# Five row chunks of 512, 512, 384, 384, 384 instead of four of 512 and one of 128, with operands moved to one offset modulo 64 bytes

## The chip, the core and the metric

The kernel runs on one core of a Trainium2 chip. The time is the device time of one execution in microseconds (us); the kernel before takes 840.11 us, the median of three runs (839.91 to 841.11). TensorE (PE) multiplies, VectorE (DVE), ScalarE (ACT) and GpSimd (POOL) work elementwise, and all DMAs are issued from SyncE (SP). A matmul on PE is a pair: a weight load (LDWEIGHTS, shown as engine PEld) of a stationary 128x128 block, and the MATMUL itself, which streams the columns of the moving operand through it.

## The reference

Four batches of 544 tokens (32 global, 512 local), eight heads of 64. Attention, then two feed-forward blocks over all 2176 tokens:

```
x  = attention(...)                      # local: window of 32 and the 32 globals; global: all keys
h  = x @ w_in                            # 512 -> 2048     "first"
g  = h * clip(h + 3, 0, 6) / 6
y  = g @ w_out                           # 2048 -> 512     "second"
h2 = max(y @ w1, y @ w2, y @ w3)         # 512 -> 768, x3  "third"
out = h2 @ w_out                         # 768 -> 512      "fourth"
```

The arithmetic is float32 where attention works on it; the four products split each operand into two fp32r parts (hi and lo) and add three products, hi·hi, hi·lo and lo·hi. The weights arrive as 64-bit floats and are decoded on the chip.

## The kernel before

Tokens are worked in chunks of rows (`CHUNKS`): four of 512, which are the local tokens of one batch each, and one of 128, the global tokens of all four batches. A product works with tokens as columns of its moving operand, so the chunk's length is the column count n of every MATMUL of the first three products: `first` and `second` issue 12 of them for each of 16 blocks f, `third` 12 for each of 18 blocks, in each chunk. That is 192, 192 and 216 pairs of load and matmul a chunk, whatever n is. `fourth` takes 18 MATMULs of 512 columns for every 128 tokens, 306 in all.

Work is recorded as operations with an engine, an assumed length, a due time and the buffers that they touch, and `Plan.order` deals them out to the engines; what it fixes is the order on each engine, no time. Attention goes by pairs of heads (`pair`) and for the global tokens by two pairs (`globals_`). Attention's results are split into the parts of x by x_hi on ACT (L337) and x_lo on DVE (L339), into tiles xt (two buffers, one batch each), and by g_hi and g_lo (L400, L402) into xg. `first` (L450) leaves each block in DRAM (gs); `second` (L538) loads it again (gr), splits it (g2: L529, L531) and sums over f in four banks; its results are the tiles y. `third` is L590, `fourth` L614, the stores L625 and L628.

`decode` loads a weight block into raw, works it on ACT (L427), DVE (L418, L420, L423) and ACT (L431), and POOL writes the low part (L432). Its results lie in two rings, w with 16 places and wx with 8: w_in's sixteen blocks take w, w_out's first eight take wx, its last eight the places of w that `first` has left. Of the last two products' 24 blocks the first eight go to w, the next eight to wx, the last eight to w.

In the program as built, the tiles w, wx, g2 and hs (the split result of `third`) begin at a multiple of 64 bytes in each partition, the tiles xt, xg and y at 32 bytes past one. All blocks inside a tile lie whole multiples of 64 bytes further on. So in `first` and `third` the moving operand (xt, xg, y) and the weights stand 32 bytes apart modulo 64; in `second` (moving g2, weights w or wx) and `fourth` (moving w, weights hs) they stand at the same offset, 0.

Of the kernel before, what the change touches and what calls it, by code (L numbers as in the profile page):

```python
# [28 lines left out]
CHUNKS = [(0, 512), (512, 512), (1024, 512), (1536, 512), (2048, 128)]  # L29
# [134 lines left out]
def body(ctx, tc, q_n, k_n, v_r, msk, msk_g, w_in, w_out, w123, w_out2, out):  # L164
# [10 lines left out]
    pools["wx"] = ctx.enter_context(P("wx", 8))  # L175
# [7 lines left out]
    tiny = const.tile([128, 1], F32, name="tiny")  # L183
    nc.vector.memset(tiny, 1.0e-9)
# [48 lines left out]
    T["wx"] = tag("wx", 8, [128, 2, 512], F32R, "wx")  # L233
# [7 lines left out]
    xT = {b: Buf(T["xt"]) for b in range(B)}  # L241
# [6 lines left out]
    def pair(b, pr, s0):  # L248
# [3 lines left out]
        xt = xT[b]  # L252
# [8 lines left out]
        for u in range(2):  # L261
# [12 lines left out]
            op("PE", 0.70, scores, s0 + 2 * u, r=[Q, K], w=sb + [(t, "held") for t in tb], what="scores")  # L274
# [28 lines left out]
            for hh in range(2):  # L303
                fb, pt = Buf(T["f"]), Buf(T["pt"])
                pts.append(pt)
                def norm(hh=hh, tb=tb, nm=nm):
                    t = tb[hh]()[:, :, 0:WIN]
                    r = nm()[:, 2, hh].rearrange("p (v o) -> p v o", o=1).to_broadcast([128, 2, WIN])
                    nc.gpsimd.tensor_tensor(out=t, in0=t, in1=r, op=ALU.mult)  # L309

                op("POOL", 1.25, norm, s0 + 2 * u + 4, r=[(nm, 2)], w=[(tb[hh], 0), (tb[hh], 1)], what="norm")
# [23 lines left out]
            op("PE", 0.9, pv, s0 + 2 * u + 7, r=pts + [V], w=[(ob, u)], what="pv")  # L335
# [3 lines left out]
        op("DVE", 0.7, lambda: nc.vector.tensor_tensor(out=xt()[:, 1, pr], in0=ob(), in1=xt()[:, 0, pr].bitcast(F32),  # L339
                                                       op=ALU.subtract), s0 + 11, r=[ob, (xt, (0, pr))],  # L340
           w=[(xt, (1, pr))], what="x_lo")

    def globals_(b, pr, g0):
# [46 lines left out]
        def g_pv():  # L390
# [9 lines left out]
        op("ACT", 0.28, lambda: nc.scalar.copy(out=xG()[:, 0, pr - 1:pr + 1, b], in_=ogv()), g0 + 10, r=[og],  # L400
           w=[(xG, (0, b, pr))], what="g_hi")
        op("DVE", 0.28, lambda: nc.vector.tensor_tensor(  # L402
            out=xG()[:, 1, pr - 1:pr + 1, b], in0=ogv(), in1=xG()[:, 0, pr - 1:pr + 1, b].bitcast(F32),
            op=ALU.subtract), g0 + 11, r=[og, (xG, (0, b, pr))], w=[(xG, (1, b, pr))], what="g_lo")

    def decode(src, into, due, rel=0.0):
# [22 lines left out]
        for i in range(3):  # L429
            op("DVE", (0.6, 0.75, 0.85)[i], lambda i=i: bits(i), due + 3, r=[R], w=[t_], what="wbits")  # L430
# [37 lines left out]
    for b in range(B + 1):  # L468
        if b < B:
            for pr in range(H // 2):  # L470
# [5 lines left out]
                s += 8 if b else 6  # L476
# [21 lines left out]
    plan.event(end_of_attention, ("att", "psS", "psF", "psO"), ("psA", "gp"))  # L498
# [22 lines left out]
    def second(c, f, due):  # L521
# [9 lines left out]
        op("DVE", 0.15 + n * .0012, lambda: nc.vector.tensor_tensor(  # L531
# [29 lines left out]
    for n in range(3 * NH + NH):  # L561
# [5 lines left out]
        W = decode(src, "wx" if 8 <= n < 16 else "w", s2 + 20 + 12 * n if n < 8 else s3 + 2.5 * (n - 8))  # L567
# [39 lines left out]
    def fourth(c, due):  # L607
# [88 lines left out]
```

## Time and profile before

| | |
|---|---|
| median of three runs | 840.11 us |
| the profiled execution: its time / its span | 840.04 / 838.3 us |
| granted TensorE clock, mean | 0.998 |
| attention alone | 0 to 53 us |
| attention and `first` together | 53 to 245 us |
| `first` alone, then with the first blocks of `second` | 245 to 354 us |
| `second` alone | 354 to 519 us |
| `second`'s chunk of 128 and `third` | 519 to 549 us |
| `third` and `fourth` | 549 to 834 us |

The span runs from the first instruction to the last; 1.7 us of the time lie outside it. The boundaries of the stages are where the first and the last MATMUL of a line start. A share of busy time of PE counts overlapping matmuls once and says nothing on how close together they are; for that the start of one group of matmuls is set against the start of the next.

### The profile page before, as it was taken

What the parts mean: (1) busy time and instruction counts of PE and PEld (TensorE: products, weight loads), DVE (VectorE), ACT (ScalarE), POOL (GpSimd) and SP (SyncE); (2) the same over time, 40 slices, a digit from 0 to 9 for tenths busy, and PEclk for the clock granted to TensorE, in tenths of its full rate; (3) what the DMA queues carried; (4) which work ended last, traced back from release to release, by engine and by line L of the source; (5) the groups of instructions that cost most, each with busy time, mean ns of one, the idle gap of its engine ahead of it and who ended that gap; (6) DMA issues with size and microseconds to landing.
All of it is one profiled execution on the core that took longest, in us unless ns stands there. A gap on an engine that the chain in (4) does not pass through costs nothing.

```text
span 838.3 us, 12516 instructions
## 1 busy us (share of the span) xinstructions
PE 822.4 (98%) x4754; PEld 671.1 (80%) x4754; DVE 374.6 (45%) x832; ACT 322.3 (38%) x754; POOL 140.2 (17%) x134
## 2 busy tenths in 40 slices
PE   6989999999999999999999999999999999999997
PEld 4767777777888888888888888988888888888897
DVE  3687878768333465643232322588122122112111
ACT  5987777776333444423232323344111111111101
POOL 2564445435000132300000001233000000000000
PEclk9999999999999999999999999999999999999999
DMA  6255746444433456643333330343100100000010
GB/s 234 69 187 191 240 125 217 160 128 152 151 115 128 134 163 202 187 144 101 94 95 101 96 94 28 99 126 100 51 1 0 38 13 0 26 26 2 13 38 13
DMA packets 53916, 85.61 MB, mean 102 GB/s; under 512 B 4576, under 2 KB 26336, under 8 KB 53856
## 3 DMA queue, kind: packets, MB, share of 16 engines
q1 hardware_dynamic: 53856, 84.81, 31.8%
q8 instruction: 37, 0.61, 0.3%
q14 instruction: 23, 0.19, 0.1%
HBM read 62.51 MB, written 22.28 MB: 101 GB/s over the span
## 4 chain that ended last, share of the span: by engine, by line
PE 96%; ACT 2%; DVE 1%; DMA 0%; POOL 0%; issue 0%; SPq 0%; ACTq 0%
PE l L450 24%; PE a L590 17%; PE a L538 16%; PE l L590 10%; PE l L538 8%; PE a L614 5%; PE f L316 4%; PE o L330 3%; PE s L271 3%; PE l L614 3%; PE s L355 1%; PE o L396 1%; ACT tbuf L284 1%; PE f L381 1%; DMA kr<-in_kn_dram 0%; ACT pt L246 0%
## 5 line engine op out<-in xcount | busy, mean ns | idle before, releaser
L450 PE MATMUL l<-xt,w 128*128 128x512 f32 x768 | 193.3, 401 | 0.0
L450 PEld LDWEIGHTS l<-xt,w 128*128 128x128 f32 x768 | 140.0, 188 | 36.1 <-issue 5.0
L531 DVE TENSOR_TENSOR g<-gr,g 128x512 fp32r<-128x512 f32 (+1 forms) x80 | 49.2, 616 | 126.0 <-ACT g L529 125.9
L529 ACT CAST g<-gr 128x512 fp32r<-128x512 f32 (+1 forms) x80 | 44.5, 558 | 137.3 <-PE a L538 70.9
L432 POOL TENSOR_TENSOR w<-wdec,w 128x512 fp32r<-128x512 f32 x40 | 54.6, 1365 | 175.2 <-ACT w L431 173.8
L456 ACT ACTIVATE ga<-l,three 128x512 f32<-128x512 f32 x80 | 49.7, 622 | 88.6 <-PE l L450 87.8
L590 PE MATMUL a<-y,w 128*128 128x512 f32 (+1 forms) x372 | 80.0, 372 | 0.0
L458 DVE SCALAR_TENSOR_TENSOR ga<-ga,l 128x512 f32<-128x512 f32 x80 | 48.3, 605 | 67.0 <-ACT ga L456 66.8
L590 PEld LDWEIGHTS a<-y,w 128*128 128x128 f32 x372 | 64.4, 188 | 13.6
L309 POOL TENSOR_TENSOR tbuf<-tbuf,nm 128x448 f32<-128x448 f32 x64 | 63.9, 1018 | 59.6 <-DVE nm L297 42.5
L538 PE MATMUL a<-g,wx 128*128 128x512 f32 (+1 forms) x336 | 69.4, 357 | 0.0
L538 PE MATMUL a<-g,w 128*128 128x512 f32 (+1 forms) x336 | 68.4, 356 | 0.0
L601 ACT CAST hs<-hm 128x512 fp32r<-128x512 f32 (+1 forms) x30 | 16.7, 556 | 125.9 <-DVE hm L599 125.9
L590 PE MATMUL a<-y,wx 128*128 128x512 f32 (+1 forms) x300 | 64.0, 371 | 0.0
L538 PEld LDWEIGHTS a<-g,w 128*128 128x128 f32 x336 | 56.2, 189 | 9.5
L538 PEld LDWEIGHTS a<-g,wx 128*128 128x128 f32 x336 | 55.9, 189 | 9.3
L284 ACT ACTIVATE tbuf<-tbuf,nm 128x224 f32<-128x224 f32 x128 | 60.4, 476 | 6.9 <-DVE nm L278 6.9
L590 PEld LDWEIGHTS a<-y,wx 128*128 128x128 f32 x300 | 51.8, 188 | 11.0
L599 DVE TENSOR_TENSOR hm<-hm,a 128x512 f32<-128x512 f32 (+1 forms) x37 | 22.6, 611 | 78.4 <-PE a L590 78.3
L432 POOL TENSOR_TENSOR wx<-wdec,wx 128x512 fp32r<-128x512 f32 x16 | 21.0, 1318 | 213.7 <-ACT wx L431 213.7
L278 DVE CUSTOM_DVE_ANT_0 tbuf<-s,mask 128x224 f32<-128x224 f32 x128 | 43.5, 384 | 22.2 <-PE s L271 20.6
L423 DVE SCALAR_TENSOR_TENSOR wdec<-raw,wdec 128x512 int32<-128x512 int32 x56 | 49.2, 879 | 1.0
(72 smaller groups left out, 1080.0 us busy)
## 6 DMA issues: line engine op xcount, KB each, us to landing
gs<-ga SPq DMA_DIRECT2D x64, 256.0 KB, 2.4
gr<-gs SPq DMA_DIRECT2D x64, 256.0 KB, 2.6
raw<-in_w_out_dram SPq DMA_DIRECT2D x22, 512.0 KB, 3.7
raw<-in_w_dram SPq DMA_DIRECT2D x18, 512.0 KB, 3.7
raw<-in_w_in_dram SPq DMA_DIRECT2D x16, 512.0 KB, 3.9
vr<-in_v_dram SPq DMA_DIRECT2D x16, 320.0 KB, 5.4
kr<-in_kn_dram SPq DMA_DIRECT2D x16, 304.0 KB, 4.8
qr<-in_qn_dram SPq DMA_DIRECT2D x16, 288.0 KB, 3.8
```

What stands on the lines that cost most here:

```text
L284: nc.scalar.activation(out=t, in_=t, func=ACTF.Exp, scale=-1.0, bias=nm()[:, 0, hh, v:v + 1], accum_out=nm()[:, 1, hh, v:v + 1])
L309: nc.gpsimd.tensor_tensor(out=t, in0=t, in1=r, op=ALU.mult)
L423: nc.vector.scalar_tensor_tensor(out=t, in0=half(0), scalar=29, in1=t, op0=ALU.logical_shift_right, op1=ALU.bitwise_or)
L432: op("POOL", 1.36, lambda: nc.gpsimd.tensor_tensor(out=flat(1), in0=t_().bitcast(F32), in1=flat(0).bitcast(F32), op=ALU.subtract), due + 5 ...
L450: nc.tensor.matmul(ps()[:, 0:n], lhsT=w[:, i, k], rhs=v, start=(k == 0 and s == 0), stop=(k == KC - 1 and s == 2))
L456: op("ACT", us, lambda: nc.scalar.activation(out=ga()[:, 0:n], in_=ps()[:, 0:n], func=ACTF.Relu, bias=three), -100, r=[ps], w=[ga], what=" ...
L458: op("DVE", us, lambda: nc.vector.scalar_tensor_tensor(out=ga()[:, 0:n], in0=ga()[:, 0:n], scalar=6.0, in1=ps()[:, 0:n], op0=ALU.min, op1= ...
L529: op("ACT", 0.16 + n * .0009, lambda: nc.scalar.copy(out=g2()[:, 0, 0:n], in_=gr()[:, 0:n]), due - 4, r=[gr], w=[(g2, 0)], what="ghi")
L531: op("DVE", 0.15 + n * .0012, lambda: nc.vector.tensor_tensor(out=g2()[:, 1, 0:n], in0=gr()[:, 0:n], in1=g2()[:, 0, 0:n].bitcast(F32), op= ...
L538: nc.tensor.matmul(A[e]()[:, 0:n], lhsT=wo[f]()[:, i, e * 128:(e + 1) * 128], rhs=g2()[:, j, 0:n], start=(f == 0 and s == 0), stop=(f == N ...
L590: nc.tensor.matmul(U[j]()[:, 0:n], lhsT=w[:, i, k], rhs=y[c]()[:, l, k], start=(s == 0), stop=(s == len(steps) - 1))
L614: nc.tensor.matmul(A[i](), lhsT=h2[c, h]()[:, p, i * 128:(i + 1) * 128], rhs=w4[h]()[:, l], start=(h == 0 and s == 0), stop=(h == NH - 1 a ...
```

## The change

`CHUNKS` becomes 512, 512, 384, 384, 384. Chunk 2 is the first 384 local rows of batch 2, chunk 3 the last 128 of batch 2 and the first 256 of batch 3, chunk 4 the last 256 of batch 3 and the 128 global rows. A head pair's result is therefore split in up to two pieces, each into the x tile of its chunk (L337/L339 become L348/L350, 24 of each in place of 16), and there are three x tiles, not two. The global rows are collected in one float32 tile xg (`g_x`) and split into chunk 4's x once, after the last of them. For room, wx has four places instead of eight, and a ring wy of four is opened where attention's space is given back: w_out's first four blocks take wx, the twelve others w as `first` leaves it; the third product's blocks 0 to 3 take w, 4 to 7 wy, 8 to 11 wx, the rest w.

A tile `pad` of 32 bytes in the constants' pool moves what is allocated on that side by 32 bytes: w, wx, wy, g2 and hs now begin at 32 past a multiple of 64 bytes, as xt and y do. In the program as built all four products have both operands at offset 32.

The planner's due times of the head pairs are set further apart (8 and then 16 where it had 6 and 8), and some of its assumed lengths are changed; these only move the order. All of the first product's chunks 3 and 4 are now due after attention.

```diff
-CHUNKS = [(0, 512), (512, 512), (1024, 512), (1536, 512), (2048, 128)]
+CHUNKS = [(0, 512), (512, 512), (1024, 384), (1408, 384), (1792, 384)]
...
-    pools["wx"] = ctx.enter_context(P("wx", 8))
+    pools["wx"] = ctx.enter_context(P("wx", 4))
...
+    const.tile([128, 8], F32, name="pad")
...
-    T["xt"] = tag("xt", 2, [128, 2, KC, SL], F32R, "lp")
-    T["xg"] = tag("xg", 1, [128, 2, KC, B, SG], F32R, "lp")
+    T["xt"] = tag("xt", 3, [128, 2, KC, 512], F32R, "lp")
+    T["xg"] = tag("xg", 1, [128, KC, B, SG], F32, "lp")
...
-        op("ACT", 0.6, lambda: nc.scalar.copy(out=xt()[:, 0, pr], in_=ob()), s0 + 10, r=[ob], w=[(xt, (0, pr))],
-           what="x_hi")
+        for c, (t0, n) in enumerate(CHUNKS):
+            i0, i1 = max(t0, b * SL) - b * SL, min(t0 + n, b * SL + SL) - b * SL
+            if i0 >= i1:
+                continue
+            at = b * SL + i0 - t0
+            xv = lambda l, c=c, at=at, m=i1 - i0: X[c]()[:, l, pr, at:at + m]
+            src = lambda i0=i0, i1=i1: ob()[:, i0:i1]
...
-                s += 8 if b else 6
+                s += 16 if b else 8
...
-        else:
+        elif b < B:
             for f in range(NF):
                 first(b - 1, f, due1)
                 due1 += 3
-                if b == B:
-                    first(B, f, due1)
-                    due1 += 1
+    c = len(CHUNKS) - 1
+    at = CHUNKS[c][1] - B * SG
+    xg = lambda: xG().rearrange("p k b q -> p k (b q)")
+    op("ACT", 0.6, lambda: nc.scalar.copy(out=X[c]()[:, 0, :, at:at + B * SG], in_=xg()), due1, r=[xG], w=[(X[c], (0, "g"))], what="g_hi")
...
+    for c in range(B - 1, len(CHUNKS)):
+        for f in range(NF):
+            first(c, f, due1)
+            due1 += 3
...
+        pools["wy"] = ctx.enter_context(P("wy", 4))
...
-        wo[f] = decode(src, "wx" if f < 8 else "w", s2 - 50 + 3 * f)
+        wo[f] = decode(src, "wx" if f < 4 else "w", s2 - 50 + 3 * f)
...
-        W = decode(src, "wx" if 8 <= n < 16 else "w", s2 + 20 + 12 * n if n < 8 else s3 + 2.5 * (n - 8))
+        W = decode(src, ("w", "wy", "wx", "w", "w", "w")[n // 4], s2 + 20 + 12 * n if n < 8 else s3 + 2.5 * (n - 8))
```

How the order moves on PE, at three places. Names: s scores, f transposes of the softmax ("flips"), o attention's output, l and a banks of the products. First the start, where attention gives way to the first matmuls of `first`. Before:

```order
L271 MATMUL s<-kr,qr 128x224 x4
L330 MATMUL o<-pt,vr 64x128 x16
L316 MATMUL f<-ident,tbuf_118 128x128 x4
L316 MATMUL f<-ident,tbuf_120 128x128 x4
L271 MATMUL s<-kr,qr 128x224 x4
L316 MATMUL f<-ident,tbuf_122 128x128 x4
L330 MATMUL o<-pt,vr 64x128 x8
L316 MATMUL f<-ident,tbuf_124 128x128 x4
L381 MATMUL f<-ident,tg 128x128 x4
L450 MATMUL l<-xt,w 128x512 x6
```

After, at the same place:

```order
L273 MATMUL s<-kr,qr 128x224 x4
L318 MATMUL f<-ident,tbuf_115 128x128 x4
L318 MATMUL f<-ident,tbuf_117 128x128 x4
L332 MATMUL o<-pt,vr 64x128 x16
L273 MATMUL s<-kr,qr 128x224 x4
L456 MATMUL l<-xt,w 128x512 x24
L273 MATMUL s<-kr,qr 128x224 x4
L456 MATMUL l<-xt,w 128x512 x6
L318 MATMUL f<-ident,tbuf_119 128x128 x4
```

Ahead of the first matmul of `first` stood 20 flips of four and 12 groups of scores; now 16 and 10, which is batch 0 and little more.

The end of `first` and the start of `second`, on PE. Before:

```order
L396 MATMUL o<-pt,vr 64x32 x20
L450 MATMUL l<-xt,w 128x512 x144
L450 MATMUL l<-xg,w 128x128 x12
L450 MATMUL l<-xt,w 128x512 x12
L450 MATMUL l<-xg,w 128x128 x12
```

After:

```order
L392 MATMUL f<-ident,tg 128x128 x5
L456 MATMUL l<-xt,w 128x384 x12
L407 MATMUL o<-pt,vr 64x32 x20
L456 MATMUL l<-xt,w 128x384 x492
L554 MATMUL a<-g_2924,wx 128x512 x12
L554 MATMUL a<-g_2935,wx 128x512 x12
L554 MATMUL a<-g_2949,wx 128x512 x12
```

Chunks of 512 and 128 alternated there, with four blocks of `second` between them further on; now 492 matmuls of 384 columns stand in a row, and `second` begins after the last.

The end of `second` and the start of `third`, on PE. Before:

```order
L538 MATMUL l<-g_4873,w 128x512 x9
L538 MATMUL a<-g_4890,wx 128x128 x12
L538 MATMUL a<-g_4907,wx 128x128 x12
L590 MATMUL a<-y_4073,w 128x512 x12
L538 MATMUL a<-g_4961,wx 128x128 x12
L538 MATMUL a<-g_4963,wx 128x128 x12
L538 MATMUL a<-g_4966,wx 128x128 x12
L538 MATMUL a<-g_5006,wx 128x128 x12
L590 MATMUL l<-y_4073,w 128x512 x12
```

After:

```order
L554 MATMUL a<-g_5185,w 128x384 x12
L554 MATMUL a<-g_5202,w 128x384 x12
L554 MATMUL a<-g_5222,w 128x384 x12
L606 MATMUL a<-y_4053,w 128x512 x12
L606 MATMUL l<-y_4053,w 128x512 x36
L606 MATMUL a<-y_4053,wy 128x512 x48
L606 MATMUL a<-y_4053,wx 128x512 x12
```

Blocks of `third` no longer stand between `second`'s last ones; `third` begins when all of them are done.

## Rows read from the trace of the kernel before

**Rows 1.** The page: granted clock in 40 slices, chain by engine.
```profile
PEclk9999999999999999999999999999999999999999
...
PE 96%; ACT 2%; DVE 1%; DMA 0%; POOL 0%; issue 0%; SPq 0%; ACTq 0%
```

**Rows 2.** What PE waited for: total us, times, longest.
```profile
PE s L271 <- DMA kr<-in_kn_dram: 4.5, 1, 4.5
PE s L271 <- DVE nm L278: 2.5, 2, 1.4
PE o L330 <- DVE xt L339: 1.0, 1, 1.0
PE f L316 <- ACT pt L246: 1.0, 1, 1.0
```

**Rows 3.** Chain of waits in order of time: start, us, engine, out, line, instructions.
```profile
429.85 44.20 PE a L538 x195
...
530.52 6.65 PE a L538 x60
...
635.83 8.40 PE l L590 x36
...
788.95 16.36 PE a L614 x72
...
810.61 6.70 PE a L590 x60
```

**Rows 4.** Timeline of PE where `first` runs alone: start us, us, instructions.
```profile
245.37 33.86 PE L450 MATMUL l<-xt,w 128*128 128x512 f32 x144
279.08 1.45 PE L450 MATMUL l<-xg,w 128*128 128x128 f32 x12
280.37 3.01 PE L450 MATMUL l<-xt,w 128*128 128x512 f32 x12
283.21 1.45 PE L450 MATMUL l<-xg,w 128*128 128x128 f32 x12
```

**Rows 5.** Timeline of PE, two short windows of one group of scores.
```profile
100.30 0.35 PE L271 MATMUL s<-kr,qr 64*128 64x224 f32 x2
...
100.68 0.35 PE L271 MATMUL s<-kr,qr 64*128 64x224 f32 x2
```

**Rows 6.** Timeline of PE and of PEld, from `first` into a flip.
```profile
142.48 0.63 PE L450 MATMUL l<-xt,w 128*128 128x512 f32 x2
142.94 0.49 PE L316 MATMUL f<-ident,tbuf 128*128 128x128 f32 x3
...
142.71 0.59 PEld L316 LDWEIGHTS f<-ident,tbuf 128*128 128x128 f32 x4
```

**Rows 7.** Timeline of PE: `first` between pieces of attention.
```profile
53.23 1.64 PE L450 MATMUL l<-xt,w 128*128 128x512 f32 x6
54.71 0.27 PE L381 MATMUL f<-ident,tg 128*128 128x128 f32 x1
...
56.96 1.66 PE L450 MATMUL l<-xt,w 128*128 128x512 f32 x6
58.55 1.36 PE L396 MATMUL o<-pt,vr 128*64 128x32 f32 x40
```

**Rows 8.** Stretches: busy PE, PEld, DVE, ACT, POOL; clock; DMA share, GB/s.
```profile
40.00:60.00 20.00, 17.40 (x204) 13.52 (x201) 16.39 (x50) 16.90 (x53) 11.22 (x10) 1.00 0.54 177
80.00:100.00 20.00, 20.00 (x163) 15.03 (x161) 18.34 (x37) 14.63 (x37) 10.87 (x10) 1.00 0.69 213
```

**Rows 9.** Groups by line and form, decode: busy us, mean ns.
```profile
L423 DVE SCALAR_TENSOR_TENSOR wdec<-raw,wdec 128x512 int32<-128x512 int32 x56 | 49.2, 879 | 1.0
L420 DVE SCALAR_TENSOR_TENSOR wdec<-raw,wdec 128x512 int32<-128x512 int32 x56 | 46.3, 827 | 1.5
...
L418 DVE TENSOR_SCALAR wdec<-wdec 128x512 int32<-128x512 int32 x56 | 36.2, 647 | 12.9 <-ACT wdec L427 12.3
```

**Rows 10.** Timeline of SP's queue at the end.
```profile
834.26 1.75 SPq L628 DMA_DIRECT2D out_dram<-hm  x4
```

More of the change, by code (lines that the diff above doesn't have):

```diff
@@ L239, in body @@
        w=[mask_g], kb=152)
-    xT = {b: Buf(T["xt"]) for b in range(B)}
+    X = [Buf(T["xt"]) for _ in CHUNKS]
     xG = Buf(T["xg"])
@@ L251, in pair @@
         held[b, pr] = S
-        xt = xT[b]
         Q, K, V = Buf(T["qr"]), Buf(T["kr"]), Buf(T["vr"])
@@ L272, in scores @@
                                          rhs=K()[o:o + 64, 128 * i:128 * i + WIN], start=True, stop=True)
-            op("PE", 0.70, scores, s0 + 2 * u, r=[Q, K], w=sb + [(t, "held") for t in tb], what="scores")
+            op("PE", 1.0, scores, s0 + 2 * u, r=[Q, K], w=sb + [(t, "held") for t in tb], what="scores")
             for v in range(2):
@@ L309, in norm @@
                     nc.gpsimd.tensor_tensor(out=t, in0=t, in1=r, op=ALU.mult)
-                op("POOL", 1.25, norm, s0 + 2 * u + 4, r=[(nm, 2)], w=[(tb[hh], 0), (tb[hh], 1)], what="norm")
+                op("POOL", 1.05, norm, s0 + 2 * u + 4, r=[(nm, 2)], w=[(tb[hh], 0), (tb[hh], 1)], what="norm")
                 def flip(hh=hh, tb=tb, fb=fb):
@@ L317, in flip @@
                                                 tb[hh]()[:, v, kb * 128:kb * 128 + 128], ident)
-                op("PE", 0.44, flip, s0 + 2 * u + 5, r=[(tb[hh], 0), (tb[hh], 1)], w=[fb], what="flip")
+                op("PE", 0.5, flip, s0 + 2 * u + 5, r=[(tb[hh], 0), (tb[hh], 1)], w=[fb], what="flip")
                 e = "DVE" if hh and u else "ACT"
-                op(e, 0.62 if e == "ACT" else 0.73, lambda e=e, pt=pt, fb=fb: copy(e, pt(), fb()), s0 + 2 * u + 6, r=[fb], w=[pt],
+                op(e, 0.6 if e == "ACT" else 0.71, lambda e=e, pt=pt, fb=fb: copy(e, pt(), fb()), s0 + 2 * u + 6, r=[fb], w=[pt],
                    what="flipped")
@@ L333, in pv @@
                                              start=(kb == 0), stop=(kb == 1))
-            op("PE", 0.9, pv, s0 + 2 * u + 7, r=pts + [V], w=[(ob, u)], what="pv")
-        op("ACT", 0.6, lambda: nc.scalar.copy(out=xt()[:, 0, pr], in_=ob()), s0 + 10, r=[ob], w=[(xt, (0, pr))],
-           what="x_hi")
-        op("DVE", 0.7, lambda: nc.vector.tensor_tensor(out=xt()[:, 1, pr], in0=ob(), in1=xt()[:, 0, pr].bitcast(F32),
-                                                       op=ALU.subtract), s0 + 11, r=[ob, (xt, (0, pr))],
-           w=[(xt, (1, pr))], what="x_lo")
+            op("PE", 0.52, pv, s0 + 2 * u + 7, r=pts + [V], w=[(ob, u)], what="pv")
+        for c, (t0, n) in enumerate(CHUNKS):
[5 more added lines that the diff above has]
+            src = lambda i0=i0, i1=i1: ob()[:, i0:i1]
+            m = i1 - i0
+            us = i0 // 256, (i1 - 1) // 256
+            op("ACT", 0.17 + m * .00083, lambda xv=xv, src=src: nc.scalar.copy(out=xv(0), in_=src()), s0 + 10,
+               r=[(ob, u) for u in us], w=[(X[c], (0, pr, b))], what="x_hi")
+            op("DVE", 0.15 + m * .00106, lambda xv=xv, src=src: nc.vector.tensor_tensor(
+                out=xv(1), in0=src(), in1=xv(0).bitcast(F32), op=ALU.subtract), s0 + 11,
+               r=[(ob, u) for u in us] + [(X[c], (0, pr, b))], w=[(X[c], (1, pr, b))], what="x_lo")
     def globals_(b, pr, g0):
@@ L399, in globals_ @@
         op("PE", 1.3, g_pv, g0 + 8, r=pts_g + [Z["V"] for Z in R], w=[og], what="g_pv")
[L400 to L404, printed above, removed]
+        op("ACT", 0.28, lambda: nc.scalar.copy(out=xG()[:, pr - 1:pr + 1, b], in_=ogv()), g0 + 10, r=[og],
+           w=[(xG, (b, pr))], what="g_x")
     def decode(src, into, due, rel=0.0):
@@ L429, in decode @@
         for i in range(3):
-            op("DVE", (0.6, 0.75, 0.85)[i], lambda i=i: bits(i), due + 3, r=[R], w=[t_], what="wbits")
+            op("DVE", (0.68, 0.82, 0.84)[i], lambda i=i: bits(i), due + 3, r=[R], w=[t_], what="wbits")
         op("ACT", 0.62, lambda: nc.scalar.copy(out=flat(0), in_=t_().bitcast(F32)), due + 4, r=[t_], w=[W], what="whi")
@@ L442, in first @@
         ps, ga = Buf(T["l"]), Buf(T["ga"])
-        x = xT[c] if c < B else xG
+        x = X[c]
         def mm(ks):
@@ L448, in mm @@
                 for s, (i, j) in enumerate(((0, 0), (0, 1), (1, 0))):
-                    v = x()[:, j, k] if c < B else x()[:, j, k].rearrange("p b q -> p (b q)")
-                    nc.tensor.matmul(ps()[:, 0:n], lhsT=w[:, i, k], rhs=v, start=(k == 0 and s == 0),
+                    nc.tensor.matmul(ps()[:, 0:n], lhsT=w[:, i, k], rhs=x()[:, j, k, 0:n], start=(k == 0 and s == 0),
                                      stop=(k == KC - 1 and s == 2))
@@ L622, in store @@
         def store(i, o):
-            if c < B:
-                row = c * NQ + SG + i * 128
-                nc.sync.dma_start(out=out[row:row + 128, :], in_=o())
+            b, p = divmod(t0 + i * 128, SL)
+            if b < B:
+                nc.sync.dma_start(out=out[b * NQ + SG + p:b * NQ + SG + p + 128, :], in_=o())
             else:
```

10 lines of the change are left out of this document (7 added, 3 removed).

## The prediction

> **What bounds the kernel now.** I read the page first, then what PE waited for, then the chain of waits in order of time. PE carries 96% of the chain and its clock is granted in full, the 2.4 GHz level, in all 40 slices [rows 1]. PE's waits that the trace names are few: 4.5 us for the first loads, and then pieces of 1.4 us at most [rows 2]. So once attention no longer stands alone, from about 53 us to the end, the time is the number of matmuls times the distance between their starts, and the question is what sets that distance. The busy share can't tell, as matmuls overlap; the chain can, since it gives for each run of matmuls its length and count [rows 3]. At 2.4 GHz a column takes 0.417 ns:
>
> - `second`, 512 columns: 44.20 / 195 = 226.7 ns, 544 cycles, 32 more than columns.
> - `fourth`, 512 columns: 16.36 / 72 = 227.2 ns, the same.
> - `third`, 512 columns: 8.40 / 36 = 233.3 ns, 560 cycles, 16 more again.
> - `first`, 512 columns alone: from 245.37 to 279.08, 33.71 / 144 = 234.1 ns, taken as 233.3 too [rows 4].
> - 128 columns: 6.70 / 60 = 111.7 ns in `third`, 6.65 / 60 = 110.8 ns in `second` [rows 3]; 268 cycles for 128 columns.
>
> Two things stand out, and the change touches both. A matmul of 128 columns costs half of one of 512, not a quarter. And `first` and `third` pay 6.6 ns a matmul that `second` and `fourth` don't; what separates the pairs in the code is that the former have their two operands 32 bytes apart modulo 64.
>
> **The change part by part.** *Columns.* The number of matmuls stays: 960, 960, 1080 and 306. Before, 768 + 768 + 864 have 512 columns and 600 have 128. After, 384 + 384 + 432 = 1200 have 512 and 576 + 576 + 648 = 1800 have 384. Before, by the rows: `third` 864 x 0.2333 + 216 x 0.1117 = 225.7 us, `first` 768 x 0.2333 + 192 x 0.1117 = 200.6 (a pair of blocks in [rows 4] takes 283.21 - 279.08 = 4.13, and 12 x (0.1117 + 0.2333) is 4.14), `second` 768 x 0.2267 + 192 x 0.1108 = 195.4: together 621.7.
>
> No row has 384 columns. At 128 the distance is the same whether the operands agree or not (111.7 and 110.8), so something else than the stream sets it, and I read it as the pace of the weight loads, one load per matmul. At 512 the loads lie under the stream and leave 32 cycles. With 384 columns the stream, 160 ns, is still longer than 111.7, so I take 384 + 32 cycles = 173.3 ns. Bounds: 170.0 if the distance goes in proportion to columns (three quarters of 226.7), 188.4 on the straight line from 111.7 to 226.7. 512 columns is the nearest row, and it leads to 173.3.
>
> *Offsets.* All operands go to 32 past 64 bytes, so weights and moving operand agree everywhere. No fp32r matmul of before has both at 32. The bounds are the two kinds of distance that it has: none of them pays the 16 cycles, or all do. I take none, for two reasons. The matmuls that are free of it are of two kinds with different tiles on either side, and agree only in the relation. And the scores, float32, have both operands at 32: from the start at 100.30 to that at 100.68 it is two steps, 0.19 us each, and 224 columns at two cycles take 0.187 [rows 5]; there is no room for another 16 cycles (6.7 ns). That is weaker than it looks, as the stream runs there at half the pace. One row speaks against it: in [rows 6] the last matmul of `first` ahead of a flip streams from offset 32 while the flip's weights load (142.71 on), and these lie at 32 too; still two matmuls take 142.94 - 142.48 = 0.46 us, 230 or more each.
>
> So after: 1200 x 0.2267 + 1800 x 0.1733 = 272.0 + 312.0 = 584.0, against 621.7: **37.7 us less** (`first` 13.7, `second` 8.5, `third` 15.5). `fourth` has the same 306 matmuls of 512 columns, at 226.7 before and after.
>
> *Order.* `first` now stands in about 50 separate places between pieces of attention, before in 44 (counted in the order). A visit costs more than its matmuls: six take 1.48 us and 1.59 us to the next start in [rows 7], where 6 x 0.2333 is 1.40; so 0.08 to 0.19 each. Six more: **1.1 us at most, taken in full.**
>
> *Start.* The first matmul of `first` has four flips and two groups of scores fewer ahead of it, so it comes earlier than 53 us and can fill waits of attention: the last three rows of [rows 2] hold 4.5 us. Against that the decode of w_in, 0.647 + 0.827 + 0.879 = 2.35 us of DVE a block [rows 9], must now keep up with fewer other steps between, and DVE is busy for 16.39 and 18.34 us of 20 in the stretches around it [rows 8]. PE idles for 20 - 17.40 = 2.6 us in the worse of these. I take 0, bounds -4.5 and +2.6.
>
> *Handovers.* Twelve of w_out's blocks, not eight, wait for `first` to leave their places. The first place comes free after block 0 of chunk 4; PE then has fifteen blocks of 12 x 0.1733 = 2.08 us and four of `second` of 2.72, 42 us. Twelve decodes need 12 x 2.35 = 28 us of DVE. Hidden; the cover is gone only if a decode takes over 42 / 12 + 2.72, some 6 us, since `second` uses a block in 2.72. The third product's blocks from 8 on follow `second`'s last chunk, 33 us long, with eight blocks of 2.72 us ready: the same picture, cost 0. [Rows 2] holds no wait of PE at either place before, so none goes away there.
>
> *Elementwise work and DMA.* x_hi and x_lo become 24 pieces each, hi and lo of the globals one step each instead of eight; a chunk of 384 has shorter steps. All of this is on ACT and DVE, beside a PE that is the bound; cost 0, and without that cover eight more steps on each. SP issues as many DMAs; the end still hangs on four stores, whose issue takes 1.75 us [rows 10], now with two larger stores just ahead of them: 0 to 0.9 us, if these two issues stand in the way, taken 0.
>
> Sum: 838.3 - 37.7 + 1.1 = 801.7 us of span; the execution's own time is 1.7 above its span (840.04), and 0.07 under the median, which I leave out: **803.4 us**. With the bounds of 384 columns below (1800 x 3.3 ns = 5.9) and of the start: 793 to 806.
>
> **The rivals.**
>
> *The moving operand's own offset costs the 16 cycles*, whatever the weights' is. Then `first` and `third` keep them and `second` and `fourth` gain them. 512 columns cost 233.3 everywhere, 384 cost 180.0: 1200 x 0.2333 + 1800 x 0.1800 = 604.0, and 306 x 6.6 ns = 2.0 for `fourth`; 15.7 saved, **825.4 us** (816 with 384 in proportion to columns). [Rows 6] speaks for it, [rows 5] against. The Trainium skill, "TensorE: Matmul & The Clock Gate", Part 2, step 1 (LDWEIGHTS), says that weights and moving operand have read ports of their own in SBUF and that the load of the next weights takes nothing from the running matmul. By that rule where the weights lie can't matter to the stream, and the time would be this rival's. The trace agrees in part: a load lies under each matmul of 512, but 32 to 48 cycles are left over, and a rule of two free ports gives no reason for them.
>
> *Chunks of 384 cost more*, on the straight line: 1200 x 0.2267 + 1800 x 0.1884 = 611.1, 10.6 saved, **830.5 us**. For it: two points are all the trace has. Against it: at 128 columns the offsets don't show, so it is another limit.
>
> *Each operand's own offset costs 16 cycles, the weights' too: slower.* 512 columns take 239.9 and 384 take 186.5 ns: 1200 x 0.2399 + 1800 x 0.1865 + 306 x 0.0132 = 627.6; 5.9 more, **847.0 us**. All 3306 matmuls are wide enough to show it. It decides from the point where the weights' offset costs (15.7 - 1.1) / 3306 = 4.4 ns a matmul on top of the rival above. Against it: the scores with both at 32 [rows 5]. The straight line together with the first rival ends there as well.
>
> *The change doesn't do what it says*: the built program's addresses show both operands at 32 in all four products, and the row counts are as said; no chance of its own.
>
> **How the numbers follow.** Forecast 0.53, moving offset 0.28, dearer 384 0.07, slower 0.07, and 0.05 for something between (a wait at a handover, half of the offsets' gain: 806 to 822). The predicted time is the first's, 803.4. Leaving out the slower case, 830.5 and the lowest corner of the first, **798 to 828** holds about 0.8. A measurement of this kernel tells 0.2% (1.7 us) from no change. Faster 0.91: the first three and the rest, less a little for losses at the start under the smaller gains; same 0.01; slower 0.08.
>
> **What would show it.** In the chain of waits after, the runs divided by their count: `second` 226.7 at 512 and 173.3 at 384, and `third` the same; 233 and 180 in both is the first rival, 240 and 187 the slower one, 188 at 384 with 226.7 at 512 the line. `first` should start before 53 us, and the waits of PE should stay in small pieces before that; a wait of PE for POOL or DVE weights (w, wx, wy) near the starts of `second` or `third` would show a handover that I count as hidden.

## The result and the profile after

| | before | after |
|---|---|---|
| median | 840.01 us (839.17 to 841.11, 4 runs) | 805.13 us (804.14 to 805.24, 4 runs) |
| span of the profiled execution | 838.3 us | 803.4 us |
| first matmul of `first` | 53.2 us | 49.1 us |
| last matmul of attention begins | 245.2 us | 246.2 us |
| `second` alone begins | 353.4 us | 331.8 us |
| `third` begins | 519.4 us | 518.7 us |
| last matmul begins | 833.2 us | 798.3 us |

The ratio is 0.9581, with a 95% interval from 0.9565 to 0.9598. The forecast was 803.4 us, with 798 to 828 as its range. A later set of runs of the same kernel gave 804.84 us.

The page of the kernel after: busy time, share and instructions of each engine, and the granted clock in 40 slices.

```profile
PE 788.2 (98%) x4754; PEld 691.8 (86%) x4754; DVE 381.6 (47%) x832; ACT 325.2 (40%) x764; POOL 141.6 (18%) x134
...
PEclk9999999999999999999999999999999999999999
```

This answers [rows 1]: PE is still the bound, and its clock is the full one (the 2.4 GHz level) but for one stretch early in attention, too short to show in a slice. The stretches there (busy PE, PEld, DVE, ACT, POOL; clock; DMA share, GB/s):

```profile
20.00:24.70 4.70, 3.31 (x21) 2.42 (x22) 2.48 (x15) 4.62 (x18) 3.11 (x4) 1.00 0.43 134
24.70:28.10 3.40, 3.31 (x17) 2.61 (x18) 2.04 (x11) 3.28 (x11) 2.04 (x3) 0.50 0.01 2
```

The granted clock falls to 0.50, the 1.2 GHz level, after 4.7 us in which PE was busy for 3.31. The profiled execution of before has no such stretch ahead of its last matmul; the one execution of the change with a mean clock of 1.000 took 804.14 us. So the gain does not come from the clock, it lies in the matmuls themselves. What PE waited for, after (total us, times, longest):

```profile
PE s L273 <- DMA kr<-in_kn_dram: 4.4, 1, 4.4
PE f L318 <- POOL tbuf L311: 1.9, 2, 1.2
PE s L273 <- DVE nm L280: 1.5, 2, 1.1
PE s L366 <- DVE nm L280: 0.8, 1, 0.8
```

Beside [rows 2], the wait for nm is shorter by 1.0 us and the one for tbuf has grown from 0.2 to 1.9 us. All of PE's waits now lie ahead of the first matmul of `first`: from 49.1 us on the list is empty, where before it still held 1.0 us behind 53.2. No wait for w, wx or wy is named, so both handovers of weight places are hidden. Now the chain of waits (start, us, engine, out, line, instructions), which answers [rows 3]:

```profile
246.45 85.48 PE l L456 x492
331.93 44.24 PE a L554 x195
419.01 33.82 PE a L554 x195
...
529.80 13.60 PE a L606 x60
...
659.90 6.24 PE l L606 x36
...
740.81 8.16 PE a L630 x36
```

Each length divided by its count is the distance from start to start:

| | columns | before [rows 3, 4] | after | forecast |
|---|---|---|---|---|
| `first` | 384 | – | 85.48 / 492 = 173.7 ns | 173.3 |
| `second` | 512 | 226.7 | 44.24 / 195 = 226.9 | 226.7 |
| `second` | 384 | – | 33.82 / 195 = 173.4 | 173.3 |
| `third` | 512 | 233.3 | 13.60 / 60 = 226.7 | 226.7 |
| `third` | 384 | – | 6.24 / 36 = 173.3 | 173.3 |
| `fourth` | 512 | 227.2 | 8.16 / 36 = 226.7 | 226.7 |

Both steps of the argument are in this table. The 16 extra cycles of `third` at 512 columns are gone, and 384 columns cost columns plus 32 cycles.

### The profile page after: what moved, and what is told of

The parts are those of the page before. It is cut to its first block, busy times and chain, and to the rows that moved or that the text cites. A ratio compares the mean times of both kernels' runs of the same rounds, so it can differ in the third digit from the quotient of the medians.

```text
span 803.4 us, 12545 instructions
## 1 busy us (share of the span) xinstructions
PE 788.2 (98%) x4754; PEld 691.8 (86%) x4754; DVE 381.6 (47%) x832; ACT 325.2 (40%) x764; POOL 141.6 (18%) x134
## 4 chain that ended last, share of the span: by engine, by line
PE 97%; DVE 1%; ACT 1%; DMA 0%; issue 0%; SPq 0%; DVEq 0%
PE l L456 24%; PE a L606 17%; PE a L554 16%; PE l L606 10%; PE l L554 7%; PE a L630 5%; PE l L630 4%; PE s L273 4%; PE o L332 4%; PE f L318 4%; PE s L366 1%; PE o L407 1%; PE f L392 1%; ACT tbuf L286 0%; DVE tbuf L280 0%; DMA kr<-in_kn_dram 0%
## 5 line engine op out<-in xcount | busy, mean ns | idle before, releaser
L456 PE MATMUL l<-xt,w 128*128 128x384 f32 (+1 forms) x960 | 201.3, 363 | 0.0
L554 PE MATMUL a<-g,w 128*128 128x384 f32 (+1 forms) x504 | 101.3, 354 | 0.0
L545 ACT CAST g<-gr 128x384 fp32r<-128x384 f32 (+1 forms) x80 | 44.5, 558 | 103.9 <-PE a L554 54.9
L547 DVE TENSOR_TENSOR g<-gr,g 128x384 fp32r<-128x384 f32 (+1 forms) x80 | 48.6, 610 | 73.4 <-ACT g L545 73.4
L464 DVE SCALAR_TENSOR_TENSOR ga<-ga,l 128x384 f32<-128x384 f32 (+1 forms) x80 | 48.4, 605 | 67.3 <-ACT ga L462 67.2
L462 ACT ACTIVATE ga<-l,three 128x384 f32<-128x384 f32 (+1 forms) x80 | 49.9, 624 | 71.9 <-PE l L456 71.1
L606 PE MATMUL a<-y,w 128*128 128x384 f32 (+1 forms) x384 | 76.7, 357 | 0.0
L280 DVE CUSTOM_DVE_ANT_0 tbuf<-s,mask 128x224 f32<-128x224 f32 x128 | 43.4, 384 | 17.7 <-PE s L273 17.6
L428 DVE SCALAR_TENSOR_TENSOR wdec<-raw,wdec 128x512 int32<-128x512 int32 x56 | 49.8, 889 | 1.4
L431 DVE SCALAR_TENSOR_TENSOR wdec<-raw,wdec 128x512 int32<-128x512 int32 x56 | 49.4, 882 | 1.2
L554 PE MATMUL l<-g,w 128*128 128x512 f32 (+1 forms) x216 | 47.1, 362 | 0.0
L606 PE MATMUL l<-y,w 128*128 128x384 f32 (+1 forms) x216 | 43.4, 356 | 0.0
```

Of the source, the lines that this page charges most:

```text
L428: nc.vector.scalar_tensor_tensor(out=t, in0=half(1), scalar=-2147483648, in1=t, op0=ALU.bitwise_and, op1=ALU.bitwise_or)
L431: nc.vector.scalar_tensor_tensor(out=t, in0=half(0), scalar=29, in1=t, op0=ALU.logical_shift_right, op1=ALU.bitwise_or)
L456: nc.tensor.matmul(ps()[:, 0:n], lhsT=w[:, i, k], rhs=x()[:, j, k, 0:n], start=(k == 0 and s == 0), stop=(k == KC - 1 and s == 2))
L462: op("ACT", us, lambda: nc.scalar.activation(out=ga()[:, 0:n], in_=ps()[:, 0:n], func=ACTF.Relu, bias=three), -100, r=[ps], w=[ga], what=" ...
L464: op("DVE", us, lambda: nc.vector.scalar_tensor_tensor(out=ga()[:, 0:n], in0=ga()[:, 0:n], scalar=6.0, in1=ps()[:, 0:n], op0=ALU.min, op1= ...
L547: op("DVE", 0.12 + n * .0011, lambda: nc.vector.tensor_tensor(out=g2()[:, 1, 0:n], in0=gr()[:, 0:n], in1=g2()[:, 0, 0:n].bitcast(F32), op= ...
```

## The experiments

In the runs below an offset pair such as (32, 0) gives the moving operand's byte offset modulo 64 first, then the weights'. The change has (32, 32) in all four products; before had (32, 0) in `first` and `third` and (0, 0) in `second` and `fourth`.

**One part alone: the chunks.** The change without `pad`; the offsets are as before.

```diff
-    const.tile([128, 8], F32, name="pad")
```

> The changed kernel without the 32-byte pad: chunks, order and buffers as changed, but weights, g2 and hs back at 0 and xt, y at 32 modulo 64. Theory (the difference of the two operands' offsets modulo 64 costs 16 cycles, 6.6 ns, a matmul): first and third at 233.3 (512) and 180.0 ns (384), second 226.7 and 173.3; (960 + 1080) x 6.6 ns = 13.5 us more than the change: 818.6 us, 21.5 less than before. Rival (places in SBUF as such, a third x buffer or the order brought what the offsets are credited with): 805 us, with 226.7 and 173.3 in all products.

Measured: 812.74 us, ratio 0.9668 (0.9654 to 0.9683). Chain of waits of this kernel, `first` and `third`:

```profile
247.69 87.11 PE l L455 x492
...
532.90 14.00 PE a L605 x60
...
655.22 10.60 PE a L605 x60
```

At 512 columns, 14.00 / 60 = 233.3 ns: the extra is back when only the offsets are taken back. At 384 it is 10.60 / 60 = 176.7 and 87.11 / 492 = 177.1 ns, so the extra is there 3.3 to 3.4 ns, half of the 6.7 that the theory took. From the start of `third`, 432 x 6.6 ns and 648 x 3.3 ns make 5.0 us; the trace has 4.9 more than the change. The end of `first` comes 2.9 us later. The expected 818.6 us was 5.9 too high. The offsets are thus worth 7.6 us under the new chunks, not 13.5; the chunks with their new order bring the other 28.

**The other part alone: the offsets.** The kernel before, with `pad` and nothing else.

```diff
+    const.tile([128, 8], F32, name="pad")
```

> The kernel before with nothing but the 32-byte pad: all operands at 32 modulo 64, chunks 4 x 512 + 128. Theory (difference of offsets): first's 768 and third's 864 matmuls of 512 columns drop from 233.3 to 226.7 ns, second and fourth stay: 10.8 us less, 829.2 us; the 128-column chunk stays at 111 to 112 ns. Rival (the moving operand's own offset): first and third stay, second's 768 and fourth's 306 rise by 6.6 ns: 7.1 us more, 847 us. Rival (the offsets matter only together with the new chunks): 840 us.

Measured: 833.08 us, ratio 0.991 (0.9895 to 0.9924), 7.7 us less than the 840.77 of before in the same set. The slower rival falls. In `third` and `fourth` the theory's gain is there: from the start of `third` to the last matmul 308.3 us instead of 313.8, 5.5 of 864 x 6.6 ns = 5.7. In `first` it is there in the long run of 144 matmuls, which by [rows 4] took 33.71 us before, from its start to the start of the next (start us, us, line, out<-in, shape, count):

```profile
245.71 32.94 PE L451 MATMUL l<-xt,w 128*128 128x512 f32 x144
278.49 1.45 PE L451 MATMUL l<-xg,w 128*128 128x128 f32 x12
```

It now takes 32.78 us, 0.93 less, where 144 x 6.6 ns is 0.95. In the short runs of `first` the gain is mostly missing. Two windows of PE's timeline show the stretch where blocks of 512 and 128 columns alternate, first before:

```profile
334.13 3.01 PE L450 MATMUL l<-xt,w 128*128 128x512 f32 x12
336.98 1.45 PE L450 MATMUL l<-xg,w 128*128 128x128 f32 x12
```

and this kernel:

```profile
333.26 3.00 PE L451 MATMUL l<-xt,w 128*128 128x512 f32 x12
336.09 1.45 PE L451 MATMUL l<-xg,w 128*128 128x128 f32 x12
```

Twelve matmuls of 512 take 2.85 us before and 2.83 with equal offsets; 12 x 6.6 ns would be 0.08. In all, from its first matmul to `second` alone, `first` becomes 2.6 us shorter (300.2 to 297.6) where 768 x 6.6 ns is 5.1. At the start 1.6 us are lost: the first matmul of `first` comes at 54.8 us instead of 53.2, with two loads waited for 1.4 us longer (kr 5.2 us, vr 0.9). So 5.5 and 2.6 less and 1.6 more make the 6.5 us by which the span is shorter (831.8). What is missing in `first` is taken up below.

**Is it the value 32, or the equality?** The pad on the other side of the memory, so that all operands of all products lie at 0.

```diff
-    const.tile([128, 8], F32, name="pad")
...
+    ctx.enter_context(P("padr", 1, side="right")).tile([128, 8], F32, name="padr")
```

> The changed kernel with the pad on the other side: xt, y and attention's tiles moved by 32 bytes to 0, weights, g2 and hs at 0 too. Theory (only the difference counts): 226.7 and 173.3 ns in all products, 805 us, as the change. Rival (32 is the better place for both, or 0 for both): off by up to 16 cycles on 3306 matmuls, 783 or 827 us.

Measured: 805.06 us, ratio 0.9576 (0.9562 to 0.959), the change's time. All runs of 512 are at 226.7 to 226.9 ns, all of 384 at 173.3 to 173.7. So equal offsets cost the same at 0 as at 32, and no operand pays for its own offset.

**The same difference the other way round.** Both pads: (0, 32) in `first` and `third`, (32, 32) in the others.

```diff
+    ctx.enter_context(P("padr", 1, side="right")).tile([128, 8], F32, name="padr")
```

> The changed kernel with pads on both sides: xt and y at 0, weights at 32 modulo 64, the opposite of before; second and fourth have both at 32. Theory (a difference in either direction costs 16 cycles): first and third at 233.3 and 180.0 ns, 13.5 us more than the change, 818.6 us. Rival (only a moving operand ahead of the weights pays): 805 us, all at 226.7 and 173.3. Rival (the moving operand alone counts, 0 is good): 805 us as well, but then the change itself would not have its 226.7 at 32.

Measured: 808.61 us, ratio 0.9619 (0.9603 to 0.9635). Chain of waits, the same three places as in the first experiment:

```profile
247.47 85.48 PE l L457 x492
...
531.05 14.00 PE a L607 x60
...
653.32 10.41 PE a L607 x60
```

512 columns pay 233.3 ns, as with (32, 0). 384 columns pay nothing: 10.41 / 60 = 173.5, 85.48 / 492 = 173.7; this is why the expected 818.6 us was 10 too high. The moving operand lies at 0 here and the weights at 32, so the rival by which the moving operand's own offset costs would have given the change's 805; it falls. The Trainium skill, "TensorE: Matmul & The Clock Gate", Part 2, step 1 (LDWEIGHTS), has it that the load of the next weights takes no read bandwidth from the running matmul, as it goes through a read port of its own. The trace speaks against this, as far as the distance between starts can: of the products' operands only the weights of `first` and `third` and both operands of the others have moved between the last two kernels, and a matmul of `third` with its moving operand at 0 goes from 226.7 to 233.3 ns with its weights at 32.

**A table of offsets and of columns.** The change, with groups of 48 equal matmuls behind the last product, one pair of offsets or one column count to a group.

```diff
+        for r in range(R): nc.tensor.matmul(probe()[:, 0:512], lhsT=wv(8), rhs=xv(0, 512), start=r == 0, stop=r == R - 1)
...
+        for r in range(R): nc.tensor.matmul(probe()[:, 0:448], lhsT=wv(0), rhs=xv(0, 448), start=r == 0, stop=r == R - 1)
```

> The changed kernel with 28 groups of 48 fp32r matmuls added behind the fourth product, all on one weight block and one y tile, read by nobody: 16 groups of 512 columns with both operands' offsets at 0, 16, 32, 48 modulo 64, and 12 groups of 128 to 448 columns with equal offsets (32, 32) and with 32 bytes between them. Theory (the difference modulo 64 counts): the four groups with equal offsets at 226.7 ns, all groups with 32 bytes between them at 233.3; whether 16 and 48 bytes pay too is open, 226.7 if pieces of 32 bytes count, 233.3 if any difference does. Columns, theory (the larger of the load's pace and columns + 32 cycles): 111.7, 111.7, 120.0, 146.7, 173.3, 200.0 ns at 128, 192, 256, 320, 384, 448, with 32 bytes between them 6.6 more from 256 up. Rival (a straight line from 128 to 512): 130.9, 150.0, 169.2, 188.4, 207.5 from 192 to 448.

Measured: 1061.5 us with the extra work, the clock at 1.00 throughout. Timeline of PE; lines 666 to 669 have the moving operand at 32 and the weights at 32, 48, 0 and 16; line 674 is (0, 32); lines 684 to 688 are equal offsets with 256, 320, 384 and 448 columns, then the first group of 128 at (0, 32):

```profile
798.15 11.04 PE L666 MATMUL l<-y,w 128*128 128x512 f32 x48
809.03 11.05 PE L667 MATMUL l<-y,w 128*128 128x512 f32 x48
819.92 11.35 PE L668 MATMUL l<-y,w 128*128 128x512 f32 x48
831.11 11.36 PE L669 MATMUL l<-y,w 128*128 128x512 f32 x48
...
886.75 11.36 PE L674 MATMUL l<-y,w 128*128 128x512 f32 x48
897.95 11.06 PE L675 MATMUL l<-y,w 128*128 128x512 f32 x48
...
985.97 5.94 PE L684 MATMUL l<-y,w 128*128 128x256 f32 x48
991.74 7.21 PE L685 MATMUL l<-y,w 128*128 128x320 f32 x48
998.78 8.48 PE L686 MATMUL l<-y,w 128*128 128x384 f32 x48
1007.11 10.07 PE L687 MATMUL l<-y,w 128*128 128x448 f32 x48
1017.02 5.47 PE L688 MATMUL l<-y,w 128*128 128x128 f32 x48
```

Starts subtracted and divided by 48 (10.88 / 48 = 226.7 for the first) give, at 512 columns in ns:

| moving at | weights at 0 | 16 | 32 | 48 |
|---|---|---|---|---|
| 0 | 226.7 | 226.9 | 233.3 | 227.1 |
| 16 | 231.9 | 233.1 | 233.1 | 232.1 |
| 32 | 233.1 | 233.3 | 226.7 | 226.9 |
| 48 | 236.3 | 226.9 | 231.5 | 231.3 |

Among 0 and 32 the relation holds. With 16 and 48 it doesn't: equal offsets cost 233.1 and 231.3 there, unequal ones 226.9 in one case. "The same offset modulo 64" is a rule for operands at 0 and 32, no more. By columns, at equal offsets: 110.6 ns at 128, 112.3 at 192, 120.2 at 256, 146.7 at 320, 173.5 at 384, 206.5 at 448. From 256 to 384 it is columns plus 32 cycles (120.0, 146.7, 173.3), below that a floor near 111, and 448 pays 6.5 ns over its 200.0. The straight line from 128 to 512 (188.4 at 384) falls, and 384 is a favourable length beside 448.

**What the order was worth.** Wider due times of the head pairs were part of the change; the prediction gave them no gain. First the change with the spacing of before.

```diff
-                s += 16 if b else 8
+                s += 8 if b else 6
```

> The changed kernel with the head pairs' old due times (6 and 8 apart instead of 8 and 16). In the order, 17 flips instead of 16 stand ahead of first, and first stands in 42 places between attention instead of 50. Theory of the prediction (the order of attention against first is worth nothing but 0.08 to 0.19 us a place): 803.5 to 805.5 us, the change being 805.1. Rival (the wider spacing is what let first start at 49 us instead of 53 and kept DVE from crowding): 807 to 810 us.

Measured: 809.95 us, ratio 0.9635 (0.9621 to 0.9648). "Worth nothing" falls; the spacing brings 4.8 us. The row of PE's waits that grew:

```profile
PE s L273 <- DVE nm L280: 6.2, 6, 2.1
```

It is 1.5 us in two pieces after the change: the next scores wait until the row maximum on DVE (L280) has read the ones before out of their bank. As other waits shrink, all named ones together grow by 3.5 us, from 10.3 to 13.8. Two pieces, of 1.8 and 2.1 us, lie among the matmuls of `first`, and 1.2 to 1.4 us behind the end of each the granted clock falls to 0.50, the 1.2 GHz level, with PE busy throughout:

```profile
82.00:85.40 3.40, 3.40 (x11) 2.71 (x12) 3.40 (x10) 0.00 (x0) 3.40 (x4) 0.50 0.19 70
116.20:119.60 3.40, 3.40 (x9) 2.56 (x9) 3.33 (x10) 2.22 (x7) 2.12 (x3) 0.50 0.35 89
```

That is one such stretch more than in the profile of the change, an estimated 1.7 us at most (half of 3.4). The two together come to the 5.2 us by which the spans differ (808.6 and 803.4). The start is not the reason, as the rival had it: `first` begins at 46.5 us here, earlier than with the change. With the pairs due closer together `first` stands in 42 places, not in 50.

**Fewer switches.** `first` issues a block's twelve matmuls as one operation, not two of six, which makes 33 visits in place of 50.

```diff
-        for ks in ((0, 1), (2, 3)):
-            op("PE", mmt(6, n), lambda ks=ks: mm(ks), 1e4 + due, r=[wi[f], x], w=[ps], what="first")
+        for ks in (range(KC),):
+            op("PE", mmt(12, n), lambda ks=ks: mm(ks), 1e4 + due, r=[wi[f], x], w=[ps], what="first")
```

> The changed kernel with each block of first as one operation of 12 matmuls instead of two of 6: first stands in 33 places between attention instead of 50. Theory (each place costs 0.1 to 0.2 us, in its first matmuls after the switch): 1.7 to 3.4 us less, 802 to 803.5 us. Rival (attention's steps wait longer for PE, up to 1.4 us each, and come late at their end): 805 to 808 us.

Measured: 808.53 us, ratio 0.9619 (0.9606 to 0.9632). No saving on switches shows in the time; the waits grew. Behind the first matmul of `first`, where PE waits for nothing after the change, it now waits for:

```profile
PE f L318 <- POOL tbuf L311: 1.2, 3, 0.6
PE l L456 <- POOL w L440: 0.5, 1, 0.5
PE s L273 <- DVE nm L280: 0.5, 1, 0.5
```

These hold 2.2 us, and the first loads (kr) took 0.5 longer, of the 3.4 us by which the kernel is slower; the rest was not taken apart. So the small pieces of six are filler for attention's waits, worth more than their switches cost.

**Wider still.** If a spacing of 16 brought 4.8 us, 24 might bring more: twice the change with another line, `s += 24 if b else 12`, and `s += 24 if b else 8`.

> The change with the due times of the head pairs set still further apart, 12 and then 24 where it has 8 and 16. Spacing 6 and 8 cost 4.9 us over the change. Theory: what the wider spacing bought is fewer waits of PE for attention's softmax (6.2 us for nm at 6 and 8, 1.5 us at 8 and 16), and of those 1.5 us and some 1.7 for tbuf are left, so at most 2 to 3 us remain to be had, while PE must have enough of the first product to put between: 802 to 805 us. Rival: attention now ends late and the third and later chunks of the first product, and w_out's decode behind them, are pushed out: over 806.5 us.

> The change with 24 in place of 16 for the head pairs of batches 1 to 3 and the 8 of batch 0 kept, so that the start is the change's. Theory: the start of the change's 8 is the better one (its first matmul of the first product comes at 49.1 us), so this is the better of the two wider spacings, 802 to 804.5 us. Rival: as above, over 806.5 us, because the order then puts attention's last pairs behind matmuls that could have waited.

Measured: 858.35 us, ratio 1.0208 (1.0192 to 1.0224), and 838.89 us, ratio 0.9982 (0.9969 to 0.9995). The theory falls by far. The second kernel's timeline of PE, `first` alone, and its stretches (busy PE, PEld, DVE, ACT, POOL; clock; DMA share, GB/s):

```profile
262.77 2.34 PE L456 MATMUL l<-xt,w 128*128 128x384 f32 x12
299.36 0.94 PE L456 MATMUL l<-xt,w 128*128 128x384 f32 x4
```

```profile
190.00:200.00 10.00, 6.64 (x68) 4.79 (x67) 2.51 (x6) 4.51 (x12) 3.64 (x4) 0.96 0.31 100
200.00:215.00 15.00, 12.74 (x83) 8.75 (x81) 4.66 (x24) 7.01 (x24) 3.65 (x4) 0.50 0.08 23
...
265.00:299.00 34.00, 23.92 (x207) 17.20 (x206) 12.15 (x53) 18.07 (x57) 9.09 (x10) 0.90 0.19 62
```

From 265 to 299 us no matmul of `first` runs, and attention alone keeps PE busy for 23.9 of 34 us; 191 to 218 is a second such gap. `first` had run dry. By PE's timeline exactly 384 of its matmuls were done when the gap at 191 began, all of chunks 0 and 1, and exactly 576 at 265, all of chunks 0 to 2; the next chunk needs rows of the batch that attention was still at work on. The first kernel has three such gaps, at 192, 384 and 576 matmuls done; the 19.5 us that it loses beyond the second were not taken apart further. In the gap at 200 the granted clock falls to 0.50, the 1.2 GHz level, after 10 us in which PE was busy for 6.6. The change leaves 492 matmuls to the end of attention, so it has filler to the last pair. The spacing of 16 lies between two losses.

**Where `first` loses part of its gain.** The change, with visits behind the last product: four flips, then 6, 12 or 24 matmuls, twelve visits of each kind; at 512 columns with offsets (32, 32) and (32, 0), then the same at 384.

```diff
+    def visit(m, d, n):
+        flips()
+        for r in range(m):
+            nc.tensor.matmul(probe()[:, 0:n], lhsT=wv(d), rhs=xv(n), start=r == 0, stop=r == m - 1)
```

> The change, with 145 short visits behind the last product: each is four flips (128 columns, float32) and then 6, 12 or 24 matmuls, twelve visits of a kind; first with 512 columns, 6 matmuls with both operands at 32, 6 with the weights at 0, then 12 and 24 likewise, and the same with 384 columns. The question is where the first product lost 1.9 us of what equal offsets and 384 columns were to bring, and where the change at the offset alone lost 2.4. Theory: the first five or six matmuls behind other work run at 229 to 233 ns whatever the offsets are, so a visit of 6 at 512 columns gains under 0.02 us from equal offsets (6 x 6.6 ns would be 0.040), a visit of 24 gains 18 x 6.6 ns, 0.12; and the second six of a visit, 12 less 6, take 1.36 us with equal offsets and 1.40 with unequal ones. Rival: equal offsets gain from the first matmul on, 0.040 for 6, 0.16 for 24, and the missing time is in the waits of attention alone.

Measured: 1278.7 us with the extra work, the clock at 1.00 throughout. Timeline of PE, the first flips of the six kinds at 512 columns and of the first three at 384, and the twelve fours of flips alone at the end:

```profile
798.43 0.60 PE L666 MATMUL l<-ident,y 128*128 128x128 f32 x4
...
820.39 0.60 PE L666 MATMUL l<-ident,y 128*128 128x128 f32 x4
...
842.46 0.60 PE L666 MATMUL l<-ident,y 128*128 128x128 f32 x4
...
880.94 0.60 PE L666 MATMUL l<-ident,y 128*128 128x128 f32 x4
...
919.79 0.60 PE L666 MATMUL l<-ident,y 128*128 128x128 f32 x4
...
990.92 0.60 PE L666 MATMUL l<-ident,y 128*128 128x128 f32 x4
...
1063.37 0.60 PE L666 MATMUL l<-ident,y 128*128 128x128 f32 x4
...
1081.21 0.60 PE L666 MATMUL l<-ident,y 128*128 128x128 f32 x4
...
1099.16 0.60 PE L666 MATMUL l<-ident,y 128*128 128x128 f32 x4
...
1270.68 5.40 PE L666 MATMUL l<-ident,y 128*128 128x128 f32 x48
```

Each difference divided by 12 is one visit: with 6 matmuls 1.830 us at equal and 1.839 at unequal offsets, with 12 3.207 and 3.238, with 24 5.928 and 6.038. Equal offsets gain:

| matmuls of a visit | gain measured | 6.6 ns each |
|---|---|---|
| 1 to 6 | 0.009 us | 0.040 |
| 7 to 12 | 0.022 | 0.040 |
| 13 to 24 | 0.079 | 0.079 |

The theory holds in kind, and the slow start is longer than the five or six that it named: it reaches into the second six, which take 1.377 us at equal offsets, 229.4 ns each, and only then 2.721 / 12 = 226.7. At 384 columns a visit of six takes 1.487 us; less the flips' 5.40 / 12 = 0.45 that is 172.8 ns a matmul, so there is no slow start there. With unequal offsets it takes 1.496, 0.009 us more. What the slow start comes from was not tested.

**The change once more**, in the set of the spacing and of the table.

> The changed kernel itself, beside the two above on the same chip: 805.1 us, so that differences of 1 to 3 us can be read.

Measured: 804.84 us, ratio 0.9574 (0.9561 to 0.9588).

## Why the prediction was right

**Columns, −37.7 with the offsets.** From the start of `second` alone to that of `third` the trace has 331.8 to 518.7, 186.9 us, and the sum's 384 x 0.2267 + 576 x 0.1733 is 186.9. From the start of `third` to the last matmul it was 313.8, with 168 matmuls of `second` of 128 columns in between (168 x 0.111 = 18.7), so 295.1; it is 279.6, the forecast's 15.5 less. The choice of 173.3 between 170.0 and 188.4 was right, and the reason given for it, a floor of 111 ns that 384 columns are clear of, agrees with the table: 110.6 at 128 and 112.3 at 192 columns. That the pace of the weight loads is this floor is not shown by any run.

**Offsets.** "Equal costs nothing" was right between 0 and 32, shown by taking the pad away (+7.6 us), by putting all at 0 (no change) and by the reverse difference (+3.5). The row that spoke against it, [rows 6], is answered by the visits: the matmuls of a run of six take 230.0 ns on average at equal and 231.5 at unequal offsets, so these two say nothing on the moving operand's own. What was wrong sits in the rivals, not in the sum: 384 columns with unequal offsets were priced at 180.0 ns and take 176.7 or 173.5. At 176.7 the first rival would have stood at 819.5 us, not 825.4.

**`first`: mis-sized by 1.9 us.** Without the four blocks of `second` that stood in it (48 x 0.2267 = 10.9), `first` was to end at 353.4 − 10.9 − 13.7 + 1.1 = 329.9 us; it ended at 331.8. The step that failed is "none pays the 16 cycles", applied to all 384 of its matmuls of 512 columns. In the order they stand in 40 visits between pieces of attention, 16 of them of twelve or more. By the table of visits 40 x 0.030 + 16 x 0.018 = 1.5 us of the offsets' gain don't come, if other pieces of attention act as flips do. The traces of the products bear this out. From its first matmul to attention's last one `first` takes 197.1 us in the change (49.1 to 246.2) and 198.2 in the first experiment (49.3 to 247.5), whose order is the same and whose offsets are those of before; PE waits for nothing in this stretch in either. So equal offsets bring 1.1 us there, where 384 x 6.6 ns is 2.5. The remaining 0.4 us was not taken apart; part of it differs from one execution to the next. In the two kernels with extra work at the end, which are the change up to there and have the full clock all the way, `second` alone begins at 331.4 and 331.6 us.

**Order, 1.1, and start, 0.** The two together came out near what was taken, but not for the reason given; that is luck. `first` starts 4.1 us earlier and attention ends 1.0 us later, and PE's named waits sum to 10.9 us before and 10.3 after. But under the new chunks with the old spacing they sum to 13.8 and the time is 4.8 us longer: the wider spacing saved what the new chunks would have cost. The prediction saw only the visits' price in it. The bounds of the start, −4.5 to +2.6, covered this.

**Handovers, elementwise work, end: 0.** No wait of PE for w, wx or wy is named. The last four stores are issued as in [rows 10], in 1.75 us:

```profile
799.37 1.75 SPq L644 DMA_DIRECT2D out_dram<-hm  x4
```

From the start of the last matmul to the end of the span it is 5.1 us before and after; the two larger stores ahead cost nothing.

**The distance to the median.** The forecast of 803.4 missed 805.13 by 1.7 us, and `first` alone has 1.9; the other terms leave 0.2 the other way.

## What to carry to other kernels

Divide the runs in the chain of waits by their counts before a change of tile sizes: a fixed 32 cycles a matmul and a floor of 111 ns showed in three rows that a last chunk of 128 columns is poor use of PE, and even chunks, with the order that goes with them, brought 28 of the 35 us. Look at the addresses of both operands of a matmul where two products of the same shape run at different distances; here 32 bytes of padding were worth 7.6 us, but test the pair of offsets, since no simple rule covered all sixteen. Short pieces of independent matmuls between dependent ones should last to the end of the dependent work: head pairs due too close together cost 4.8 us, and running out of them cost 34.

## What the runs showed of the hardware

- A difference of 32 bytes between the two operands costs 6.6 ns at 512 columns in both directions. At 384 it costs 3.3 ns with the moving operand at 32 in the products, and nothing the other way. In the visits, where the same weights and columns are used again and again, (32, 0) at 384 costs 0.009 us in the first six matmuls and nothing later (behind the first twelve, 12 further ones take 2.08 us at equal and at unequal offsets). Why is open.
- With the moving operand at 16 or 48, equal offsets cost 231 to 233 ns; the best partner of 48 is 16 (226.9), and 16 has none (231.9 at best).
- 448 columns cost 206.5 ns, 6.5 over columns plus 32 cycles, at equal offsets and at (0, 32) alike.
- After flips the first six matmuls of 512 columns take 230.0 ns on average and the second six 229.4, and only then 226.7; at 384 columns there is no such start.
- The granted clock fell to 0.50, the 1.2 GHz level, just after waits of PE of 1.8 and 2.1 us with the old spacing, and with a spacing of 24 at 200 us, after 10 us in which PE was busy for 6.6.
